# Two linear-attention and two gated-MLP layers on one Trainium2 core: K of layer two at one Strassen level, and a new order of the first loads, heads and prologues

## The chip, the cores and the metric

The kernel runs on one core of one Trainium2 chip. The metric is the device time of one execution in microseconds (us); the time of a kernel is the median of its runs. The core has five engines that the text names: TensorE (PE; its weight loads are PEld), VectorE (DVE), ScalarE (ACT), GpSimd (POOL) and SyncE (SP), which here issues every DMA. Matmuls write to PSUM, which has eight banks of 128 x 512 f32; everything else lies in SBUF, which the program holds as one tensor called `arena` (and PSUM as `ps`).

## The reference

S = 2048 tokens, D = 1024, 32 heads of 32, F = 3584. A is a linear attention without a mask, B a gated MLP without a nonlinearity, and each is applied twice with the same weights.

```python
def A(x, wqkv, wo):
    q, k, v = heads(x @ wqkv)
    phi = lambda t: jnp.where(t > 0, t + 1, jnp.exp(t)) + 1e-6
    pq, pk = phi(q), phi(k)
    kv = jnp.einsum("bhsd,bhse->bhde", pk, v)
    z = jnp.einsum("bhsd->bhd", pk)
    num = jnp.einsum("bhqd,bhde->bhqe", pq, kv)
    den = jnp.einsum("bhqd,bhd->bhq", pq, z)[..., None] + 1e-6
    return merge(num / den) @ wo

def B(x, w_gate, w_up, w_down):
    return ((x @ w_gate) * (x @ w_up)) @ w_down

x = x + A(layernorm(x)); x = x + B(layernorm(x))
x = x + A(layernorm(x)); x = x + B(layernorm(x))
```

## The kernel before, in words

All of x stays in SBUF as 16 token tiles of 128 (`x_res`, bf16). A layer norm is split over the engines (class `LN`, L508): statistics (L471 and L473 on VectorE, or L465 and L483 on ScalarE), the root on POOL (L474 and L476, or L467, L485 and L487), the scaled tile (L504 or L497 on VectorE), and the transposition into `xnT`, by TensorE with a copy of ScalarE (L596 and L598; L588 and L590 for tile 0) or by a DMA (L582). `flow_step` moves each of these on by one tile.

`layer_A` (L937) does attention in three stages. In the K and Q stage each tile of 128 tokens gets its K and Q: 8 matmuls of 512 columns for each half of 512 features. ScalarE takes the exponential of a PSUM bank (L657 in layer one, L1031 and L1027 in layer two), VectorE takes its minimum with 1 (L647 for K, L645 for Q) and joins it with the linear part (L662; L1040 and L1050 in layer two). For K, POOL then adds the tile to the sum z (`z_add`, L971, instructions L976 and L978). The G stage (L1291) multiplies normalized x by phi(K) over all tokens, and the stage with L1303, L1331 and L1383 makes V, the output projection and the residual.

In layer one K and Q use plain matmuls (L954), in the order of the list `seq`. The first two tiles do K only; in tiles 2 to 5 Q of the tile two back goes ahead of K, from tile 6 on K goes ahead of Q. Beside the K tiles from the fourth on, VectorE forms four sums of Q's weight blocks (`pt_ops`, L821 at 128 x 2048), which a DMA stores in `pt_scratch` for layer two.

In layer two `kq_pairs` (L997) works by pairs of token tiles. Every step has a position, and the steps are emitted in the order of their positions (L1173 to L1200). K is plain for all eight pairs (L945): four steps of 8 matmuls. Q is at one Strassen level for seven pairs (`strassen`, L1100; matmuls L1115): seven products of 4 matmuls in place of the eight of a plain pair. `st1` copies product 1 to a second bank (L1124), `st5` stores product 5 (L1130), `st6` and `st7` add that to a bank on VectorE (`join`, L1119), and each finished bank gets its phi. The Strassen products need sums of token blocks, which VectorE makes for two pairs at a time (`s_sums`, L1080, through L821 at 128 x 1024), and sums of weight blocks, which are loaded from `pt_scratch` (`load_t`). The phi of a step is emitted in that step. K uses banks 0 to 3 and Q banks 4 to 7, apart from the first pair.

Every engine's queue is in order. What reads and writes which bytes or banks is tracked by a recorder (`_Prog`), which puts a semaphore wait on each instruction that needs one; nothing is reordered after emission. So the order on each queue, SP's with its DMAs too, is the order in which the Python code emits.

`layer_B` (L1438) multiplies by gate, up and down weights with one Strassen level and, for some products, two (L1470, L1540, L2020, L1918; joins L1559). A part of the first pair's products, the prologue `pro`, is emitted ahead of the stage by `pro_step` (L1432), which pops one matmul group each time. In layer two one group goes between the last two output groups of attention (L1415), and in the second pass three go into product 3 of the down projection (L1952). Layer one has no prologue for its first pass (L1726).

## Time and profile before

| what | value |
|---|---|
| median of 3 runs | 1447.18 us (1445.64 to 1447.40) |
| the profiled execution's own time | 1446.97 us |
| its span, first to last instruction | 1445.2 us |
| instructions | 21993 |
| mean granted TensorE clock | 1.000 |
| DMA moved | 324.41 MB, mean 224 GB/s |
| K and Q stage of layer two, L945's start to L1291's | 98.3 us |

The profile page gives the busy time of each engine, the span in slices, the DMA queues, the chain of work that ended last and the costliest groups. `L945` is line 945 of the kernel before. In a timeline a row reads: start, length, engine, line, operation, out<-in, shape, count, and in brackets the idle time of the engine before it with what ended it. In a group row the figures after the bar are busy time, mean nanoseconds of one, and idle time before it. A row of waits reads: who waited for whom, us in total, times, the longest. A row of windows gives the length and, for PE, PEld, DVE, ACT and POOL, busy us and count, then the clock, the DMA share and GB/s. A row of DMA issues gives count, size of each and median us from issue to landing.

### The profile page before, as it was taken

Reading aid. Unit: us, or ns where it says so; the run is one execution under the profiler, and the core shown is the slowest. Engines: PE = TensorE matmul, PEld = TensorE weight load, DVE = VectorE, ACT = ScalarE, POOL = GpSimd, SP = SyncE. Lnnn points to the kernel's source line nnn. Section 1 sums busy time; section 2 is a strip of 40 time slices with the busy share of each in tenths; the row PEclk is TensorE's granted clock in tenths of the full one; section 3 lists DMA queues with packets and bytes.
Section 4 is the critical chain, followed back from the end, with each engine's and each line's share of the span. In section 5 each row is a group of like instructions: output and inputs, shape, how many; then the busy total and the mean of one; then the engine's idle time right before and its main releaser. Section 6 shows DMA issues by size and latency. Waiting matters only on the chain.

```text
span 1445.2 us, 21993 instructions
## 1 busy us (share of the span) xinstructions
PE 1433.9 (99%) x8294; PEld 800.4 (55%) x8294; DVE 1128.6 (78%) x2027; ACT 680.2 (47%) x1438; POOL 227.5 (16%) x260
## 2 busy tenths in 40 slices
PE   8999999999999999999999999999999999999999
PEld 3444444555544555554664444456666457666547
DVE  6766889889867799877677779879877786777856
ACT  3652256677720255550156423567777005777401
POOL 4543733000000000000044346300000000000000
PEclk9999999999999999999999999999999999999999
DMA  6334757987879899986896067679975779887657
GB/s 233 88 79 118 151 125 155 290 298 249 294 288 338 262 271 294 293 257 225 253 341 195 0 173 151 155 213 274 282 260 197 241 247 296 264 264 257 205 164 239
DMA packets 377993, 324.41 MB, mean 224 GB/s; under 512 B 178208, under 2 KB 326048, under 8 KB 377632
## 3 DMA queue, kind: packets, MB, share of 16 engines
q1 hardware_dynamic: 377888, 323.02, 74.5%
q8 instruction: 65, 1.06, 0.3%
q14 instruction: 40, 0.33, 0.1%
HBM read 237.24 MB, written 62.13 MB: 207 GB/s over the span
## 4 chain that ended last, share of the span: by engine, by line
PE 92%; DVE 4%; DMA 2%; ACT 1%; issue 0%; SPq 0%; POOL 0%; DVEq 0%
PE ps L1470 25%; PE ps L1540 17%; PE ps L2020 16%; PE ps L1291 8%; PE ps L954 6%; PE ps L1383 6%; PE ps L1918 6%; PE ps L945 4%; PE ps L1115 3%; DVE arena L821 2%; DVE arena L824 1%; DMA arena<-in_A_wqkv_dram 1%; DMA arena<-in_B_w_up_dram 1%; DMA arena<-in_B_w_down_dram 1%; PE ps L1303 0%
## 5 line engine op out<-in xcount | busy, mean ns | idle before, releaser
L821 DVE TENSOR_TENSOR arena<-arena 128x512 f16<-128x512 f16 (+7 forms) x752 | 414.1, 577 | 75.9 <-ACT arena L1584 47.6
L1470 PE MATMUL ps<-arena 128*128 128x512 f16 x1808 | 446.5, 379 | 0.7 <-ACT ps L1500 0.7
L824 DVE SCALAR_TENSOR_TENSOR arena<-ps,arena 128x512 f16<-128x512 f32 (+2 forms) x448 | 298.8, 686 | 76.0 <-PE ps L2020 52.2
L1540 PE MATMUL ps<-arena 128*128 128x256 f16 x2324 | 311.8, 273 | 1.7 <-DVE ps L1559 1.3
L1540 PEld LDWEIGHTS ps<-arena 128*128 128x128 f16 (+1 forms) x2324 | 226.2, 98 | 105.0 <-DVE ps L1559 5.8
L1470 PEld LDWEIGHTS ps<-arena 128*128 128x128 f16 (+1 forms) x1808 | 176.4, 98 | 141.8 <-ACT ps L1500 1.4
L2020 PE MATMUL ps<-arena 128*128 128x512 f16 (+1 forms) x1120 | 243.2, 379 | 0.0
L2020 PEld LDWEIGHTS ps<-arena 128*128 128x128 f16 x1120 | 109.6, 98 | 131.3
L1475 ACT ACTIVATE arena<-ps 128x512 f16<-128x512 f32 x224 | 134.0, 598 | 94.0 <-PE ps L1470 90.8
L1556 ACT COPY ps<-ps 128x256 f32<-128x256 f32 x220 | 81.1, 369 | 128.5 <-PE ps L1540 121.4
L1559 DVE TENSOR_TENSOR ps<-ps,arena 128x256 f32<-128x256 f32 x220 | 92.3, 428 | 36.5 <-PE ps L1540 18.4
L474 POOL TENSOR_SCALAR arena<-arena 128x1 f32<-128x1 f32 x48 | 19.5, 407 | 626.1 <-DVE arena L473 626.1
L954 PE MATMUL ps<-arena 128*128 128x512 bf16 x512 | 112.5, 379 | 3.8 <-DMA arena<-in_A_wqkv_dram 1.1
L1291 PE MATMUL ps<-arena 128*128 128x512 bf16 x512 | 115.4, 379 | 0.0
L1383 PE MATMUL ps<-arena 128*128 128x512 bf16 x512 | 111.0, 379 | 0.0
L1922 ACT COPY ps<-ps 128x256 f32<-128x256 f32 x32 | 11.4, 357 | 209.2 <-PE ps L1918 147.1
L1214 POOL TENSOR_TENSOR arena<-arena 128x1024 f16<-128x1024 f32 x32 | 79.2, 2476 | 70.2 <-DVE arena L1212 69.0
L1500 ACT COPY ps<-ps 128x512 f32<-128x512 f32 x112 | 64.2, 573 | 52.0 <-PE ps L1540 44.5
L1918 PE MATMUL ps<-arena 128*128 128x256 f16 (+1 forms) x784 | 87.0, 273 | 0.1
L978 POOL TENSOR_TENSOR arena<-arena 128x512 f32<-128x512 f32 x60 | 74.8, 1266 | 74.1 <-DVE arena L1040 44.0
L954 PEld LDWEIGHTS ps<-arena 128*128 128x128 f16 x512 | 49.5, 98 | 63.0 <-DMA arena<-in_A_wqkv_dram 1.6
L1383 PEld LDWEIGHTS ps<-arena 128*128 128x128 f16 x512 | 50.1, 98 | 60.2
(77 smaller groups left out, 1215.6 us busy)
## 6 DMA issues: line engine op xcount, KB each, us to landing
arena<-w_scratch SPq DMA_DIRECT2D x84, 512.0 KB, 4.9
arena<-sp_scratch SPq DMA_DIRECT2D x56, 512.0 KB, 5.8
arena<-t_scratch SPq DMA_DIRECT2D x29, 896.0 KB, 6.8
arena<-in_B_w_down_dram SPq DMA_DIRECT2D x21, 896.0 KB, 6.9
w_scratch<-arena SPq DMA_DIRECT2D x28, 512.0 KB, 6.5
sp_scratch<-arena SPq DMA_DIRECT2D x28, 512.0 KB, 4.1
arena<-in_B_w_gate_dram SPq DMA_DIRECT2D x42, 256.0 KB, 5.0
arena<-in_B_w_up_dram SPq DMA_DIRECT2D x42, 256.0 KB, 3.2
```

What stands on the lines that cost most here:

```text
L821: P.add("dve", lambda e: e.tensor_tensor(out=out, in0=a, in1=b, op=op), rd=rd, wr=wr, prd=prd)
L824: P.add("dve", lambda e: e.scalar_tensor_tensor(out=out, in0=a, scalar=sc, in1=b, op0=ALU.mult, op1=op1), rd=rd, wr=wr, prd=prd)
L954: return [e.matmul(psb(bank), xnT[:, k, i * 128:(i + 1) * 128], w[:, k, :], start=(k == 0), stop=(k == KT - 1)) for k in range(KT)]
L1291: return [e.matmul(psb(bank), xr[:, t, j * 128:(j + 1) * 128], pk[:, h, t, :], start=(t == 0), stop=(t == NST - 1)) for t in range(NST)]
L1383: return [e.matmul(psb(bank), xnT[:, g, i * 128:(i + 1) * 128], wp[:, g, dh * 512:(dh + 1) * 512], start=(dh == 0 and g == 0), stop=(g == ...
L1470: P.add("pe", lambda e: [e.matmul(psb(bank), w[:, k, :], x[:, k, :], start=(start and k == 0), stop=(k == 3), skip_group_check=True) for k ...
L1475: P.add("act", lambda e: e.activation(t, psb(bank), AF.Copy, scale=SG), prd=[bank], wr=r)
L1540: P.add("pe", lambda e: [e.matmul(psb(bank)[:, 256 * half:256 * half + 256], w[:, k, :], xx[:, k, :], start=(start and k == 0), stop=(k == ...
L1556: P.add("act", lambda e: e.copy(psb(dst[c])[:, 0:256], lo), prd=[bk], pwr=[dst[c]])
L1559: P.add("dve", lambda e: e.tensor_tensor(out=psb(dst[c])[:, 256:512], in0=lo, in1=c5, op=ALU.add), prd=[bk], rd=rc5, pwr=[dst[c]])
L1918: P.add("pe", lambda e: [e.matmul(psb(bank)[:, 256 * half:256 * half + 256], a[:, k, :], w[:, k, :], start=(start and k == 0), stop=(k == ...
L2020: return [e.matmul(psb(bank), hv[:, 7 * hf + k, t * 128:(t + 1) * 128], w[:, k, :], start=(start and hf == 0 and k == 0), stop=(hf == 1 an ...
```

## The change

- **First loads.** x tile 1 is loaded ahead of K's weights, and two tiles come ahead of the second half of Q's weights.
- **Early heads.** In layer one tiles 0 and 1 no longer go through `seq`. Their K is emitted by hand: half of tile 0's first half, the transposes of tile 1, the rest, tile 1's first half, the transposes of tile 2, then the second halves. Half of tile 1's statistics stands ahead of tile 0's scaling. From tile 2 on K always goes ahead of Q.
- **K at one Strassen level.** `KSTR` is on and `KP0` is 3, so pairs 3 to 7 of K go through `strassen`, with their phi by halves (`SEP = "qk"`). Layer one also forms and stores the sums of K's weights (`pt_ops("k")`, at tiles 9 to 13), and layer two loads them behind Q's. The second block of Q's plain weights, which only the last tiles use, is loaded behind the stage. The positions of Q, of the norm and of the sums are other ones; the sums for a pair stand earlier. There are three exponential buffers in place of four.
- **Phi one step later.** In `kq_pairs` the phi of a step (`fin1`, `fin2`) is put on a list and emitted behind the next K or Q step; the list is emptied ahead of the first step of a pair.
- **Prologues earlier.** Layer one's first pass gets a prologue of one group (`P1A` of pair 0), three output groups ahead of the end of attention. In layer two's first pass three groups go between the last output groups, and in the second pass four.

In numbers: 20 matmuls of 512 columns fewer (196 to 336 at L1115, 288 to 128 at L945); on VectorE 14 to 24 joins, 15 to 6 double phi (L1040), 30 to 48 single phi (L1050), 31 to 22 minima of 1024 and 2 to 20 of 512 (L647), 16 to 20 sums of 128 x 2048; on ScalarE 12 copies L1130 in place of 7, and 5 copies L1124 without a bias more.

```diff
-    KSTR = False
-    QLAG = 0.284
-    QEND = 0.102
-    SEP = "q"
-    LNP = (0.474, 0.5)
-    SPOS = 0.283
-    SSTEP = 0.14
+    KSTR = True
+    NEB = 3
+    KQ_SEQ = ""
+    QLAG = 0.409
+    QEND = 0.476
+    SEP = "qk"
+    LNP = (0.371, 0.594)
+    SPOS = 0.874
+    SSTEP = 0.119
...
-    KP0 = 1
+    KP0 = 3
...
             for h in range(2):
+                if h and mid is not None:
+                    mid()
                 P.add("dve", (lambda h: lambda e: e.bn_stats(...
...
-                OP5 = {"k": RC, "q": RC + 2048 if KSTR else RC + 2 * SZ_SLOT + 4096}
+                OP5 = {"k": RC, "q": RE + 6144 if KSTR else RC + 2 * SZ_SLOT + 4096}
...
+                pend, left = [], {}
+
+                def flush():
+                    while pend:
+                        pend.pop(0)()
...
-                def fin2(kind, i, eb, b0, b1, up):
+                def fin2(*a):
+                    pend.append(lambda: fin2_(*a))
+
+                def fin1(*a):
+                    pend.append(lambda: fin1_(*a))
...
-                            at(((p - SPOS if p else 0.05) if KSTR else p + 1 - SPOS) + SSTEP * n, f)
+                            at((p - SPOS if KSTR and p >= KP0 else p + 1 - SPOS) + SSTEP * n, "S%d%d" % (p, n), f)
...
-                for _, _, f in sorted(ev, key=lambda t: t[:2]):
-                    f()
+                for _, _, tk, f in run:
+                    if tk[0] not in "KQ":
+                        f()
+                        continue
+                    if tk[2] == "0":
+                        flush()
+                    n = len(pend)
+                    f()
+                    for _ in range(min(n, len(pend))):
+                        pend.pop(0)()
+                flush()
...
                 lnp.start(0)
-                lnp.b_one()
-                lnp.start(1)
+                lnp.start(1, lnp.b_one)
...
-            seq = [("k", i) for i in range(NHOLD)]
+            seq = []
             for i in range(NHOLD, NST):
-                pair = [("k", i), ("q", i - NHOLD)]
-                seq += pair[::-1] if first and i < NPE_T else pair
-            if not first:
+                seq += [("k", i), ("q", i - NHOLD)]
+            if first:
+                b0, b1, b2, b3 = next_banks(4)
+                kq_i[0] += 4
+                ev = [phi_evac(b, [k_dst(i, h) for h in range(2)]) for i, b in enumerate(((b0, b1), (b2, b3)))]
+                proj_kh(0, 0, b0, range(4))
+                lnp.step_t(1)
+                proj_kh(0, 0, b0, range(4, KT))
+                ev[0][0](0)
+                lnp.b_one()
+                lnp.start(3)
+                proj_kh(1, 0, b2)
+                ev[1][0](0)
+                lnp.step_t(1)
+                for i, b in enumerate((b1, b3)):
+                    proj_kh(i, 1, b)
+                    ev[i][0](1)
+                    ev[i][1]()
+                    z_add(i)
+                lnp.b_one()
+                lnp.start(4)
+            else:
                 kq_pairs()
                 seq = []
...
+                if not first and i == NST - 1:
+                    pro_step(pro, 1)
                 y_grp(tok[i], 0, i)
...
                 y_seed(i + 1)
+                if i == NST - 2 or not first and i == NST - 1:
+                    pro_step(pro, 1)
...
-                if i == NST - 1:
-                    pro_step(pro, 1)
                 y_grp(tok[i], 1, i)
...
-                npro = 0 if jit else [tk[:2] in early for _, tk in seq].index(False)
+                npro = [tk[:2] in early for _, tk in seq].index(False)
+                if jit:
+                    npro = 1
+                    seq.insert(0, seq.pop([tk for _, tk in seq].index("P1A+")))
...
-                            if q == "3" and i in (3, 4) and (i == 4 or p):
+                            if q == "3" and i in (3, 4):
                                 pro_step(pro, 1)
...
                     elif t == 1:
                         if KSTR:
-                            load_t("k", 0, 2)
+                            load_q(1, 1)
                     elif t == 2:
-                        if KSTR:
-                            load_t("k", 2, 2)
-                        else:
+                        load_t("q", 0)
+                        if not KSTR:
                             load_q(0, 0)
                             load_q(1, 0)
-                        load_q(1, 1)
-                        load_t("q", 0)
+                            load_q(1, 1)
                     else:
                         load_t("q", 1, 2)
                         load_t("q", 3)
-                        if not KSTR:
+                        if KSTR:
+                            load_t("k", 0, 2)
+                            load_t("k", 2, 2)
+                        else:
                             load_q(0, 1)
...
+        xload(1)
         load_w("k", 0)
-        xload(1)
+        xload(2)
         load_w("k", 1)
-        xload(2)
+        xload(3)
         load_w("q", 0)
-        xload(3)
+        xload(4)
+        xload(5)
         load_w("q", 1)
-        for i in range(4, NST):
+        for i in range(6, NST):
             xload(i)
```

More of the change, by code (lines that the diff above doesn't have):

```diff
@@ L533, in buf, with start @@
                 return n % 4 if (n < 10 if self.to == "B" else n >= 8) else n % 2
-            def start(self, i):
+            def start(self, i, mid=None):
                 assert i == self.n
                 act = self.stat_act
-                j = ln_a(self.order[i], act, self.o_junk)
+                j = ln_a(self.order[i], act, self.o_junk, mid)
                 self.n += 1
@@ L947, in proj2, with proj @@
                       rd=r_xT(i * 128, (i + 1) * 128) + rw[0] + rw[1], pwr=[bank])
[L949 to L951 removed]
+            def proj(w, rw, i, bank=None, ks=range(KT)):
+                if bank is None:
+                    bank = B_KQ[kq_i[0] % len(B_KQ)]
+                    kq_i[0] += 1
                 def fn(e):
                     return [e.matmul(psb(bank), xnT[:, k, i * 128:(i + 1) * 128], w[:, k, :],
[L955 removed]
+                                     start=(k == 0), stop=(k == KT - 1)) for k in ks]
                 P.add("pe", fn, rd=r_xT(i * 128, (i + 1) * 128) + rw, pwr=[bank])
@@ L966, in q_dst, with proj_kh @@
                 return x_res[:, i, h * 512:(h + 1) * 512], r_x(i, h * 512, (h + 1) * 512)
-            def proj_kh(i, h):
-                proj(wkh[first][h], R(O_WKH[first][h], 8192), i)
+            def proj_kh(i, h, bank=None, ks=range(KT)):
+                proj(wkh[first][h], R(O_WKH[first][h], 8192), i, bank, ks)
             def z_add(i):
@@ L1010, in bk @@
                 def bk(kind, p):
-                    r = ROLE[0 if kind == "k" and (p < KP0 or not KSTR) else p % 2]
+                    r = ROLE[0 if kind == "k" else p % 2]
                     return {n: BG["q" if p == 0 else kind][r[n]] for n in r}
```

63 lines of the change are left out of this document (37 added, 26 removed).

## The prediction

> **What bounds the kernel now.** I read the page's busy shares and its chain first, then TensorE's waits, then single stretches of the timelines.
>
> ```profile
> PE 1433.9 (99%) x8294; PEld 800.4 (55%) x8294; DVE 1128.6 (78%) x2027; ACT 680.2 (47%) x1438; POOL 227.5 (16%) x260
> PE 92%; DVE 4%; DMA 2%; ACT 1%; issue 0%; SPq 0%; POOL 0%; DVEq 0%
> ```
>
> TensorE (PE) is busy 99% of the span and holds 92% of the chain that ended last. So time changes in two ways only: fewer matmuls, or fewer and shorter gaps between them. Two pieces of the chain in order of time (start, length, line, count) price a matmul, and TensorE's own waits (total, times, longest) show the gaps; the others stand in the parts below.
>
> ```profile
> 737.16 10.51 PE ps L945 x48
> 835.48 6.91 PE ps L1291 x32
> PE ps L1115 <- DVE ps L1119: 0.2, 1, 0.2
> ```
>
> A 512-column matmul takes 6.91/32 = 0.216 us when nothing stops it. Idle time is counted from a modelled end (a row's last matmul lasts 379 ns), so each gap costs 379 - 216 = 0.16 us more than the rows show: 1.15 is 1.31 lost. The K and Q stage of layer two runs from 737.16 to 835.48, 98.3 us. It holds 256 plain and 196 Strassen matmuls, 452 x 0.216 = 97.6; only 0.7 us of it is gaps.
>
> **Part 1: the start of layer one (loads with x first, early heads).** The timeline, the issues and the chain from the start:
>
> ```profile
> 7.93 1.90 PE L954 MATMUL ps<-arena 128*128 128x512 bf16 x8 [0.94 <-ACT arena L590]
> 10.98 1.90 PE L954 MATMUL ps<-arena 128*128 128x512 bf16 x8 [1.15 <-DMA arena<-in_A_wqkv_dram]
> 12.72 0.61 PE L596 MATMUL ps<-arena 128*128 128x128 f16 x8
> 14.47 3.63 PE L954 MATMUL ps<-arena 128*128 128x512 bf16 x16 [1.15 <-ACT arena L598]
> 25.29 0.61 PE L596 MATMUL ps<-arena 128*128 128x128 f16 x8
> 5.77 0.55 DVE L504 TENSOR_SCALAR arena<-arena 128x1024 f16<-128x1024 bf16 x1 [1.00 <-POOL arena L476]
> 13.41 1.01 ACT L598 COPY arena<-ps 128x1024 f16<-128x1024 f16 x1
> arena<-in_A_wqkv_dram SPq DMA_DIRECT2D x1, 1024.0 KB, 5.5
> arena<-in_A_x_dram SPq DMA_DIRECT2D x1, 256.0 KB, 5.8
> 2.80 8.13 DMA arena<-in_A_wqkv_dram
> 1.71 0.43 SPq L433 DMA_DIRECT2D arena<-in_A_wqkv_dram  x1
> 2.18 0.58 SPq L433 DMA_DIRECT2D arena<-in_A_x_dram  x1
> 3.10 1.42 DVE L471 BATCH_NORM_STATS2 arena<-arena 128x6 f32<-128x512 bf16 x2 [3.10 <-DMA arena<-in_A_x_dram]
> ```
>
> Two gaps of 1.31 us follow the first half-projection: the second half of K's weights lands at 10.93, and tile 1 waits for its transposed copy. Nothing else is queued on TensorE to fill them.
>
> Loads land in the order of issue: K's first half, issued 1.71, lands at 7.2; x tile 1, issued 2.18, at 8.0; K's second half at 10.93. A tile is about 0.8 us of queue, 1 MB about 2.9. With tile 1 ahead, it lands about 0.8 us behind tile 0 (3.10), near 4.0, and K's first half near 8.0, 0.1 us later than TensorE needs it (7.93). K's second half, behind one more tile, lands near 11.7.
>
> On VectorE (DVE) half of tile 1's statistics (0.71) moves into the 1.0 us in which L504 waits for GpSimd (POOL): no cost if tile 1 has landed by 5.0. The rest of tile 1's chain then ends with L504 about 2.5 us after tile 0's, at 8.8. TensorE: four matmuls 8.0 to 8.9, transposes of tile 1 to 9.3 (about 0.45, from the 12.72 row and its successors), four matmuls to 10.2, then a wait for the copy (0.7 after the transposes' start, 1.01 long) to 10.65. Then tile 1's first half to 12.4, transposes of tile 2 to 12.8, both second halves to 16.3, K of tile 2 to 19.75, transposes of tile 3, Q of tile 0 to 23.65. Before, the same work (with the transposes that start at 25.29) ends at 25.74. **Gain 2.1 us**; bounds: 2.6 with both gaps wholly gone, 0 if later weights and the copy give as much back. Q's halves (near 15.4 and 19.8) are needed at 20.2 and 21.9.
>
> ```profile
> 61.87 2.32 PE L954 MATMUL ps<-arena 128*128 128x512 bf16 x10 [0.55 <-DVE arena L662]
> 51.81 1.80 DVE L821 TENSOR_TENSOR arena<-arena 128x2048 f16<-128x2048 bf16 x1
> 81.47 0.55 DVE L497 TENSOR_SCALAR arena<-arena 128x1024 f16<-128x1024 bf16 x1 [2.46 <-POOL arena L487]
> ```
>
> The gap at 61.87 (0.55 + 0.16) has its origin where the old order put K of tiles 5 and 6 back to back; the new order alternates from the start, so Q's eviction gets 3.45 us more. I count **0.7 us** (bounds 0 and 0.7). Layer one also makes K's four weight sums: four L821 of 1.80 us, for tiles 9 to 12, and a 2 MB store. In these tiles VectorE waits 2.46 us for GpSimd anyway, so they cost nothing; were that cover gone, at most 4 x 1.8 on VectorE. SP's store goes out two tiles (13.8 us) before V's load queues behind it.
>
> **Part 2: a prologue product earlier at the start of layer one's MLP.**
>
> ```profile
> 243.89 0.82 PE L1470 MATMUL ps<-arena 128*128 128x512 f16 x3 [0.67 <-ACT ps L1500]
> 283.25 0.83 PE L1540 MATMUL ps<-arena 128*128 128x256 f16 x6 [0.74 <-DVE ps L1559]
> 260.48 4.62 DVE L821 TENSOR_TENSOR arena<-arena 128x256 f16<-128x256 bf16 x10 [1.34 <-DMA arena<-in_B_w_up_dram]
> ```
>
> P1A's four matmuls go 24 matmuls ahead, so its copy (L1500) is done and the 0.83 us at 243.89 goes. But what is late next is VectorE, which runs on weight loads here (1.34 us at 260.48) and holds TensorE at 283.25. VectorE's order is unchanged, so TensorE reaches 283 earlier and waits longer. I count **0**; bounds 0 and -0.8.
>
> **Part 3: K of layer two.** Pairs 3 to 7 go from 32 to 28 matmuls: 5 x 4 x 0.216 = **4.3 us** less, all on TensorE's path. What this adds lies on the other engines:
>
> ```profile
> 736.90:780.00 43.10, 42.87 (x199) 19.05 (x197) 32.13 (x48) 30.96 (x56) 24.77 (x34) 1.00 0.89 274
> 780.00:835.50 55.50, 55.50 (x258) 25.02 (x257) 39.64 (x58) 25.25 (x43) 20.36 (x18) 1.00 0.18 56
> L1050 DVE SCALAR_TENSOR_TENSOR arena<-ps,arena 128x512 bf16<-128x512 f32 x15 | 10.3, 688 | 4.1 <-ACT arena L1027 3.9
> L1040 DVE SCALAR_TENSOR_TENSOR arena<-ps,arena 128x1024 bf16<-128x1024 f32 x7 | 8.6, 1224 | 0.2
> L1119 DVE TENSOR_TENSOR ps<-ps,arena 128x512 f32<-128x512 f32 x8 | 5.5, 689 | 0.0
> L647 DVE TENSOR_SCALAR arena<-arena 128x1024 bf16<-128x1024 bf16 x6 | 2.5, 422 | 1.9 <-ACT arena L1031 1.8
> L645 DVE TENSOR_SCALAR arena<-arena 128x512 bf16<-128x512 bf16 x4 | 1.2, 291 | 6.1 <-ACT arena L1031 6.1
> ```
>
> From 780 VectorE is busy 39.64 of 55.5 us, 9.25 per pair of steps (60 matmuls, 12.95 us). A Strassen pair of K loses 2 x (0.42 + 1.22) = 3.3 us of phi and gets 4 x (0.29 + 0.69) and two joins of 0.69, 5.3: VectorE's pair becomes 11.25 us, TensorE's 56 x 0.216 = 12.1. ScalarE, busy 25.25 of 55.5 us, gets two copies more per pair. So VectorE goes to 93%, with the sums (L821) unevenly in pairs 3 and 5, where it is over 100% for some microseconds. A join has 2.6 us (three other steps of 0.86) until TensorE needs it, 0.9 of it its own; a lag of over 1.7 us stalls TensorE. For it speaks that phi is now queued one step later: before, VectorE sat in front of phi for ScalarE (6.1 us before L645, 4.1 before L1050) with a join behind. Against it is a collision on GpSimd:
>
> ```profile
> 830.92 1.22 DVE L647 TENSOR_SCALAR arena<-arena 128x512 bf16<-128x512 bf16 x1 [0.67 <-ACT arena L1031]
> 829.72 2.27 POOL L978 TENSOR_TENSOR arena<-arena 128x512 f32<-128x512 f32 x2 [2.83 <-DVE arena L1040]
> ```
>
> A half phi minimum, 0.29 us alone, took 1.22 beside the z sum and ended 0.15 us after it. K's tiles now end 1.73 us apart and a z sum lasts 2.27, so about one minimum per pair is caught: 0.93 us, VectorE's pair 12.2, against 12.1. I take gaps of 1.1 us for the stage in place of 0.7: **-3.9 us**. Bounds: -5.0 with no gap; three catches per pair (14.0 on VectorE, 5 x 1.9 lost) +4.7.
>
> [...]
>
> The loads: K's four blocks (2 MB) go ahead of the stash and the transposes, Q's last block (0.5 MB) goes behind the stage. The queue is full:
>
> ```profile
> arena<-pt_scratch SPq DMA_DIRECT2D x1, 1024.0 KB, 9.5
> 759.57 1.49 SPq L582 DMA_TRANSPOSE arena<-arena  x1
> arena<-arena SPq DMA_TRANSPOSE x1, 3.8
> ```
>
> 1.5 MB more at the start's 2.9 us per MB, and one reload of 0.25 MB more ahead, is about 5.1 us: the fourth transpose (759.57 + 3.8) lands near 768.5 instead of 763.4. The sums for pair 4 now need it at step position 3.13, 737.2 + 12 x 1.73 + 13 x 0.86 = 769.1, and VectorE arrives 1 to 2 us later: no cost, with 1.6 to 2.6 us to spare. Past that each microsecond stalls VectorE, joins behind it.
>
> **Part 4: prologue of layer two's MLP.**
>
> ```profile
> 961.76 1.92 PE L1540 MATMUL ps<-arena 128*128 128x256 f16 x14 [0.55 <-DVE ps L1559]
> 963.83 1.49 PE L1540 MATMUL ps<-arena 128*128 128x256 f16 x12
> 1203.26 1.92 PE L1540 MATMUL ps<-arena 128*128 128x256 f16 x14
> 1205.33 1.48 PE L1540 MATMUL ps<-arena 128*128 128x256 f16 x12
> ```
>
> Product 1's three steps now stand between groups of eight 0.216 us matmuls, so the join wait at 961.76 (0.71) goes, and of the 0.55 lost inside each block (2.07 for 14 x 0.108) the second join, 0.2. **-0.9 and -0.2** (bounds: 0 and -1.6 together). Between the two places TensorE's waits show nothing of this size, so nothing late swallows it.
>
> **Sum.** -2.1 - 0.7 + 0 - 3.9 - 0.9 - 0.2 = -7.8 us. The profiled execution took 1446.97 us (span 1445.2 and 1.8 around it), 0.2 under the median of the three runs, 1447.18. Forecast from the median: **1439.4 us**.
>
> **Rivals.**
> - VectorE becomes the bound of pairs 3 to 7 by collisions with GpSimd (slower). It breaks even where 5 x (11.25 + 0.93 n - 12.1) = 7.8 + 1.1, at n = 2.8 catches of the five minima in a pair. At all five VectorE needs 15.9 us a pair, 19 us lost less the 1.1 counted: 1457. For: the 1.22 row. Against: GpSimd is busy only 20.36 of 55.5 us. Chance 0.06, slower in two thirds of it.
> - Most of the Strassen gain goes into gaps behind late joins or the late transpose: 3.4 us more, 1442.8. For: 93% on VectorE, in-order. Chance 0.2.
> - The start gains nothing, because the first weights or tile 1 land later: 1441.5. Chance 0.1.
> - Part 2's gap is also won, and the stage has no gaps: 1437.5. Chance 0.12.
> - Forecast: 0.52, between 1438.3 and 1441.
>
> 0.2% (2.9 us) is about what a measurement of this kernel can tell from no change. Faster (below 1444.3): 0.52 + 0.2 x 0.9 + 0.1 + 0.12 = 0.92, taken as 0.89 since the rows come from one execution. Same 0.07, slower 0.04. The range 1436.8 to 1443.4 leaves out the first rival and the outer parts of two others.
>
> **What would show it.** Start: no wait of L954 for weights, Q of tile 0 done near 23.7. No gap near 60. At 280 a gap of 1.5 us or more (mine) or under 1 (the fourth rival). L945 to L1291 of 94.4 us; L1119 as releaser of at most 1.1 us, and L647 at 512 columns with a mean under 0.55. No gap of 0.5 near 955. I am wrong if that stage exceeds 96 us, or if the start keeps a gap over 1 us.

## The result, and the profile after

The changed kernel takes **1442.07 us** (median of 5 runs, 1441.05 to 1442.24) against 1447.18 (1445.64 to 1449.32, 5 runs) before: a ratio of 0.9961, 95% interval 0.9948 to 0.9975. It is faster by 0.4%. The forecast was 1439.4 us: the sign is right and the time lies in the range, 2.7 us above the forecast. The profiled execution took 1442.1 us, with a span of 1440.0.

The busy shares and the shares of the chain that ended last, from the page of the changed kernel:

```profile
PE 1430.2 (99%) x8274; PEld 799.4 (56%) x8274; DVE 1144.7 (79%) x2059; ACT 686.1 (48%) x1448; POOL 230.0 (16%) x260
PE 95%; DVE 2%; DMA 2%; SPq 0%; ACT 0%; issue 0%
```

TensorE has 20 matmuls fewer and still bounds the kernel. To see where the 5.2 us of span come from, one lays the same piece of work of the two chains side by side. First the kernel before (start, length, engine, line, count):

```profile
117.29 6.91 PE ps L1291 x32
...
252.42 8.03 DMA arena<-in_B_w_up_dram
...
270.92 7.62 DMA arena<-in_B_w_down_dram
...
1120.26 48.36 PE ps L2020 x224
```

Then the changed kernel, where L1291, L2020 and L945 have become L1349, L2083 and L949:

```profile
116.01 6.91 PE ps L1349 x32
...
250.87 8.59 DMA arena<-in_B_w_up_dram
...
269.90 8.20 DMA arena<-in_B_w_down_dram
...
736.70 10.36 PE ps L949 x48
...
830.92 6.91 PE ps L1349 x32
...
1115.05 48.36 PE ps L2083 x224
```

Up to the G stage of layer one the change wins 1.28 us (117.29 to 116.01). Up to the K and Q stage of layer two it gives 0.82 back: that begins at 736.70 in place of 737.16, only 0.46 earlier. The stage itself is 94.22 us long in place of 98.32: 4.10 won. Layer two's MLP prologue brings 0.65 more (1120.26 to 1115.05 is 5.21), and the rest nothing. The chain shows where the second step loses: it runs over the same two weight loads as before, and both take longer from issue to landing, 8.59 in place of 8.03 us (w_up) and 8.20 in place of 7.62 (w_down). That is 1.14 us together, against 0.27 won on the way from the G stage to the first of them.

TensorE's timeline shows each part of the change (start, length, line, shape, count, and in brackets the idle time ahead with what ended it):

```profile
8.23 1.18 PE L959 MATMUL ps<-arena 128*128 128x512 bf16 x4 [1.27 <-DMA arena<-in_A_wqkv_dram]
...
10.05 3.91 PE L959 MATMUL ps<-arena 128*128 128x512 bf16 x12
...
257.26 0.83 PE L1600 MATMUL ps<-arena 128*128 128x256 f16 x6 [0.41 <-DVE ps L1619]
261.85 1.47 PE L1530 MATMUL ps<-arena 128*128 128x512 f16 x6 [0.52 <-ACT arena L1535]
282.80 0.83 PE L1600 MATMUL ps<-arena 128*128 128x256 f16 x6 [1.29 <-DVE ps L1619]
...
784.02 6.22 PE L1140 MATMUL ps<-arena 128*128 128x512 f16 x28 [0.56 <-DVE ps L1144]
...
958.62 1.49 PE L1600 MATMUL ps<-arena 128*128 128x256 f16 x12 [0.43 <-ACT arena L1644]
```

The gaps of the old start and the one at 61.87 are gone. The odd row is 10.05: 12 matmuls that should take 12 x 0.216 + 0.16 = 2.75 us take 3.91, with no wait between them. The gap at 243.89 is gone too, but there are two new ones at 257 and 262, and the one at 283 has grown from 0.74 to 1.29.

Why the start came short is in the windows (length; busy us and count of PE, PEld, DVE, ACT, POOL; TensorE's granted clock; DMA share; GB/s):

```profile
5.60:9.00 3.40, 1.54 (x13) 0.87 (x13) 2.07 (x5) 1.07 (x2) 0.90 (x3) 0.99 1.08 366
9.00:12.40 3.40, 3.40 (x16) 1.74 (x14) 1.98 (x4) 1.41 (x2) 0.79 (x2) 0.50 1.09 356
```

For 3.4 us, from 9.0 to 12.4, the granted clock was 0.50, and the 5 matmuls of 512 columns that started from 10.05 to 11.76 stood 0.427 us apart in place of 0.216. Four of the five runs have a mean clock of 0.999.

### The profile page after: what moved, and what is told of

Its sections match the earlier page's. It is cut to its first block, busy times and chain, and to the rows that moved or that the text cites. A ratio compares the mean times of both kernels' runs of the same rounds, so it can differ in the third digit from the quotient of the medians.

```text
span 1440.0 us, 22015 instructions
## 1 busy us (share of the span) xinstructions
PE 1430.2 (99%) x8274; PEld 799.4 (56%) x8274; DVE 1144.7 (79%) x2059; ACT 686.1 (48%) x1448; POOL 230.0 (16%) x260
## 4 chain that ended last, share of the span: by engine, by line
PE 95%; DVE 2%; DMA 2%; SPq 0%; ACT 0%; issue 0%
PE ps L1530 26%; PE ps L1600 17%; PE ps L2083 16%; PE ps L959 8%; PE ps L1441 8%; PE ps L1349 8%; PE ps L1981 6%; PE ps L1140 5%; PE ps L949 2%; DVE arena L825 1%; DVE arena L828 1%; DMA arena<-in_B_w_up_dram 1%; DMA arena<-in_B_w_down_dram 1%; PE ps L1361 0%; PE ps L1389 0%; DMA arena<-in_A_wqkv_dram 0%
## 5 line engine op out<-in xcount | busy, mean ns | idle before, releaser
L825 DVE TENSOR_TENSOR arena<-arena 128x512 f16<-128x512 f16 (+8 forms) x756 | 419.6, 581 | 76.9 <-ACT arena L1644 47.6
L2083 PE MATMUL ps<-arena 128*128 128x512 f16 (+1 forms) x1120 | 243.2, 379 | 0.0
L2083 PEld LDWEIGHTS ps<-arena 128*128 128x128 f16 x1120 | 109.6, 98 | 131.3
L1349 PE MATMUL ps<-arena 128*128 128x512 bf16 x512 | 115.4, 379 | 0.0
L1441 PE MATMUL ps<-arena 128*128 128x512 bf16 x512 | 111.5, 379 | 0.0
L983 POOL TENSOR_TENSOR arena<-arena 128x512 f32<-128x512 f32 x60 | 78.8, 1334 | 65.6 <-DVE arena L1073 34.0
L1441 PEld LDWEIGHTS ps<-arena 128*128 128x128 f16 x512 | 50.1, 98 | 59.8
```

Of the source, the lines that this page charges most:

```text
L825: P.add("dve", lambda e: e.tensor_tensor(out=out, in0=a, in1=b, op=op), rd=rd, wr=wr, prd=prd)
L1349: return [e.matmul(psb(bank), xr[:, t, j * 128:(j + 1) * 128], pk[:, h, t, :], start=(t == 0), stop=(t == NST - 1)) for t in range(NST)]
L1441: return [e.matmul(psb(bank), xnT[:, g, i * 128:(i + 1) * 128], wp[:, g, dh * 512:(dh + 1) * 512], start=(dh == 0 and g == 0), stop=(g == ...
L2083: return [e.matmul(psb(bank), hv[:, 7 * hf + k, t * 128:(t + 1) * 128], w[:, k, :], start=(start and hf == 0 and k == 0), stop=(hf == 1 an ...
```

## The experiments

Theory after the result: the terms of the forecast hold at full clock. What is missing at the end is (a) the stretch at half clock at the start, (b) the landing of the second w_down load near 278, which VectorE waits for and TensorE behind it, and which is not the same in every execution. Rivals: the start's order, or the new prologue, or a VectorE that is too full, costs the time by the way the code is ordered. All kernels below are edits of the changed kernel, and each was also run several times beside the kernel before on the same chip, except the one without the z sum, which has one time. In most profiles of the experiments some 50 matmul records are missing, so their starts and releasers are read, not their counts.

| kernel | median us (range, runs) | ratio to before, 95% interval |
|---|---|---|
| changed, once more | 1440.56 (1439.82 to 1441.40, 5) | 0.9955 [0.9942, 0.9969] |
| dummy matmuls at the start | 1442.00 (1439.24 to 1443.32, 5) | 0.9955 [0.9942, 0.9967] |
| no prologue in layer one | 1441.39 (1439.90 to 1441.98, 5) | 0.9952 [0.9940, 0.9965] |
| old start | 1443.58 (1442.08 to 1444.27, 6) | 0.9968 [0.9956, 0.9980] |
| phi not delayed | 1445.97 (1443.93 to 1447.65, 11) | 0.9986 [0.9978, 0.9995] |
| K plain (no Strassen for K) | 1445.34 (1442.79 to 1446.88, 11) | 0.9980 [0.9971, 0.9989] |
| six pairs of K at Strassen | 1443.81 (1441.51 to 1446.34, 8) | 0.9973 [0.9963, 0.9984] |
| no z sum in layer two | 1441.58 (1) | |
| early w_down loads | 1441.20 (1440.60 to 1442.45, 5) | 0.9961 [0.9948, 0.9973] |
| early w_down and dummies | 1439.57 (1438.74 to 1440.87, 5) | 0.9948 [0.9935, 0.9960] |
| the same, no prologue | 1440.46 (1439.40 to 1441.35, 5) | 0.9948 [0.9935, 0.9962] |
| early w_down, dummies, six pairs | 1440.75 (1440.39 to 1443.71, 5) | 0.9958 [0.9946, 0.9971] |

Differences of 1 us between two of these lie inside the intervals, so the traces decide. The second table cuts every trace at the first matmul of a stage (us): A from the first projection to the G stage, B from there to the K and Q stage of layer two, of that B' the piece from V's last stage (L1441, or L1383 before) to the first down projection, C the K and Q stage of layer two.

| trace | first projection at | A | B | B' | C |
|---|---|---|---|---|---|
| before | 7.93 | 109.19 | 619.87 | 221.22 | 98.33 |
| changed | 8.23 | 107.62 | 620.70 | 222.04 | 94.22 |
| changed, once more | 8.22 | 106.36 | 620.04 | 221.38 | 94.01 |
| dummies | 8.65 | 106.36 | 621.74 | 223.09 | 94.08 |
| no prologue | 8.61 | 106.36 | 620.55 | 221.89 | 94.70 |
| old start | 7.92 | 109.32 | 620.35 | 221.69 | 95.03 |
| phi not delayed | 8.40 | 107.62 | 619.45 | 220.80 | 98.22 |
| K plain | 8.12 | 106.37 | 619.47 | 220.81 | 97.56 |
| six pairs | 8.69 | 107.61 | 619.26 | 220.62 | 97.39 |
| no z sum | 8.59 | 107.61 | 620.90 | 222.24 | 93.50 |
| early w_down | 8.59 | 107.60 | 619.29 | 220.63 | 94.45 |
| early w_down, dummies | 9.55 | 106.36 | 619.10 | 220.45 | 94.66 |
| the same, no prologue | 8.25 | 106.36 | 618.84 | 220.18 | 95.41 |
| the three together | 8.32 | 106.36 | 618.59 | 219.94 | 96.25 |

### The start: dummies, the old start, and the same kernel again

```diff
                 lnp.start(1, lnp.b_one)
                 lnp.step_t(1)
+                P.add("pe", lambda e: [e.matmul(psb(B_KVT[1]), wrm[:, 0:128], wrm, start=True, stop=True) for _ in range(5)],
+                      rd=R(O_A[0], 1024), pwr=[B_KVT[1]])
```

> Adds five unused 512-column matmuls on TensorE between the transposes of tile 0 and the first K matmuls, where the changed kernel's TensorE sits idle from 6.8 to 8.2 us. Theory (the start lost 1.1 us because TensorE's clock was cut to half from about 9.0 to 12.4 us, after a stretch that was mostly idle): clock 1.000 over the span in every run, no 427 ns spacing between matmuls near 10 to 12.5, the G stage starts near 114.8 in place of 115.84, 1441.0 us. Rival (the slow stretch comes from loads landing beside the matmuls, or hits at random whatever TensorE does): the half clock stays, 1442.1.

The old start puts the old order of loads and the old `seq` back (and takes out the K steps of tiles 0 and 1 that were emitted by hand):

```diff
...
-            seq = []
+            seq = [("k", i) for i in range(NHOLD)]
             for i in range(NHOLD, NST):
-                seq += [("k", i), ("q", i - NHOLD)]
+                pair = [("k", i), ("q", i - NHOLD)]
+                seq += pair[::-1] if first and i < NPE_T else pair
...
+        load_w("k", 0)
         xload(1)
-        load_w("k", 0)
+        load_w("k", 1)
         xload(2)
-        load_w("k", 1)
...
```

> Undoes the loads with x first and the early heads, all else as changed. Theory (the two together gave 1.28 us: 0.6 in the start and 0.7 from the gap at 61.87, which came from K of tiles 5 and 6 standing back to back): both 1.31 us gaps and the gap near 62 are back, clock 1.000, the G stage starts near 117.1, 1443.4. Rival (the gap near 62 depended on something else that changed, and the start lost more than it won): no gap near 62, 1442 or less.

The changed kernel was also run again without an edit.

> The changed kernel once more, nothing edited. Theory (what TensorE loses between 240 and 290 us is set by when the second w_down load lands, and that landing differs from execution to execution): the profiled execution shows another gap near 283 than the 1.45 us of the first one, anywhere from 0.2 to 3, and the load's time from issue to landing differs from 8.20 us by several tenths; the stretch from the G stage's first matmul to the K and Q stage of layer two differs from 620.70 by up to 1.3 us. Rival (the gap belongs to the order of the code): the gap is again 1.45 within 0.2 and the stretch 620.7 within 0.3. Either: median 1441.0 to 1442.5, K and Q stage of layer two 94.2 within 0.5.

Its median, 1440.56, is below the expected 1441.0 to 1442.5; the gap near 283 and the w_down load follow in the next part. A takes only two values with the new start, 106.36 and 107.6, and 1.25 us lies between them. The windows of the second execution of the same code are the test:

```profile
5.60:9.00 3.40, 1.82 (x13) 1.08 (x13) 2.10 (x5) 1.07 (x2) 0.96 (x3) 1.00 1.05 366
9.00:12.40 3.40, 3.16 (x22) 1.53 (x20) 1.95 (x4) 1.51 (x2) 0.79 (x2) 1.00 1.09 358
```

The same instructions, now at a clock of 1.00, and A is 1.26 us shorter. So the code alone does not bring the half clock. It was there in 5 of the 8 profiled executions that have the new start without dummies and in none of the 4 with them. The mean clock of a run, which has three digits, points the same way: 1.000 in 19 of 20 runs with dummies and in 22 of 51 runs of the kernels with the new start and without them (1.25 us is one thousandth of the span). In 52 runs of the kernel before on the same chips it was 1.000 in 32, though its profile and that of the old start show A without a half clock; what lowers it in the others no trace shows.

Each trace also records when the clock rises. In all 14 the first matmuls, from 1.36 us on, stand about 0.43 us apart until the record of full clock begins, which is between 4.50 and 6.89 us: at 5.55 and 6.89 in the two executions of the changed kernel. (Ahead of that the windows read 1.00 because nothing is recorded.) The 3.41 us from the rise, for the changed kernel, its second execution and the dummies:

```profile
5.55:8.96 3.41, 1.55 (x13) 0.86 (x13) 2.03 (x5) 1.07 (x2) 0.94 (x3) 1.00 1.08 366
6.89:10.30 3.41, 2.43 (x22) 1.33 (x19) 2.24 (x6) 1.65 (x3) 0.79 (x2) 1.00 1.08 370
5.07:8.48 3.41, 2.08 (x15) 0.85 (x13) 1.95 (x4) 1.07 (x2) 1.36 (x4) 1.00 1.06 371
```

TensorE's busy time in this stretch sorts all 14 traces. In the five that lose the clock right behind it, for the next 3.41 us, it is 1.17 to 1.55 us; in the nine that keep it, before and the old start among them, it is 1.85 to 2.48. With the new start and no dummies the rise comes at 4.64 to 5.55 us in the five and at 6.51 to 6.89 in the other three, late enough for the stretch to take in more of the first projection. With the dummies it comes at 4.50 to 5.65, mostly as early as in the five, and the clock stays. So with the new start the clock fell where the kernel had no dummies and the rise came at 5.55 us or earlier, in five traces of five, and in none of the other seven. Why the rise moves, and whether the busy time itself decides, no trace shows.

The length of 3.41 us is read from the profiled execution of the changed kernel: its windows have a clock of 1.00 from 5.55 to 8.96, 0.50 from 8.96 to 12.37, and 1.00 from 12.37 to 16.00. TensorE was not wholly idle ahead of the fall: it was busy 1.55 us there, and 1.17 to 1.55 of the 3.41 us in the five traces.

The dummies' median did not fall by the 0.8 to 1.3 us that the start won: B is 621.74 in that trace, the longest of all. That is the next question. With the old start all three gaps are back (1.44 and 1.31 at 11.1 and 14.6, 0.71 at 62.0, counted with the modelled 0.16) and A of 109.32.

### Where 0.8 to 2.5 us go between 240 and 290

```diff
-                npro = [tk[:2] in early for _, tk in seq].index(False)
-                if jit:
-                    npro = 1
-                    seq.insert(0, seq.pop([tk for _, tk in seq].index("P1A+")))
+                npro = 0 if jit else [tk[:2] in early for _, tk in seq].index(False)
```

> Undoes the earlier prologue group of layer one's first MLP pass alone. Theory (TensorE waits near 283 for VectorE, which hangs on DMA landings, whatever it does before): the 0.83 us gap near 242 comes back, the gaps near 257, 262 and 283 (0.57, 0.68 and 1.45 us) shrink by as much, 1442.1, within 0.4. Rival (the earlier group itself made the 0.83 us that this stretch lost): the down projection starts 0.8 us earlier, 1441.2.

Without the prologue the gap of 0.83 is back at 241.74, the one at 257 is gone, the one near 262 is down to 0.2 and the one near 282 to 1.3 (0.57, 0.68 and 1.45 in the changed kernel, all with the modelled 0.16). B' is 221.89 in place of 222.04, so the rival's 0.8 us is not there. The median is 0.7 below the expected one, and so outside its 0.4; all five of its runs have a mean clock of 1.000.

VectorE's timeline near 276, first of the changed kernel, then of its second execution, then with the dummies:

```profile
278.12 2.62 DVE L825 TENSOR_TENSOR arena<-arena 128x1024 f16<-128x1024 bf16 x4 [1.99 <-DMA arena<-in_B_w_down_dram]
```

```profile
275.97 2.62 DVE L825 TENSOR_TENSOR arena<-arena 128x1024 f16<-128x1024 bf16 x4 [1.25 <-DMA arena<-in_B_w_down_dram]
```

```profile
277.97 2.62 DVE L825 TENSOR_TENSOR arena<-arena 128x1024 f16<-128x1024 bf16 x4 [3.45 <-DMA arena<-in_B_w_down_dram]
```

In all three VectorE is done with its work and sits until the second w_down load has landed. The chains give that load's time from issue to landing: 8.20, 7.54 and 8.49 us, and 7.01 with phi not delayed, where the edit is 450 us later:

```profile
269.79 7.01 DMA arena<-in_B_w_down_dram
```

The same load at the same place of the same queue takes 7.0 to 8.5 us, and TensorE's gap near 282 follows: 0.26, 0.72, 1.45 and 2.92 us (with 0.16 for the modelled end). Between the two executions of the changed kernel nothing differs but the execution, so the code does not fix this gap. With the dummies the load was also issued late: the SP queue took 6.59 us (262.86 to 269.45) for what stands ahead of it, 5.36 in the second execution. Moving the load is the test:

```diff
-                    elif u % 4 == 0:
-                        if j:
-                            wd_store(j - 1)
-                        if j < NJ // 2:
-                            wd_load(j)
+                    elif u % 4 == 3:
+                        if j + 1 < NJ // 2:
+                            wd_load(j + 1)
+                    elif u % 4 == 0:
+                        if j:
+                            wd_store(j - 1)
+                        else:
+                            wd_load(0)
```

> Changed kernel with each w_down load after the first issued one product earlier in layer one's first pass, behind the sums that read the buffer and ahead of the weight loads and the store that it stood behind. Theory (the second w_down load at 278 holds VectorE and through it TensorE, and swallows what is won before it): VectorE's wait for w_down near 278 (1.99 us) and the gap near 283 (1.45) go; the stretch from the G stage to the K and Q stage of layer two falls from 620.7 to 619.2 to 619.8, the median to about 1440.8. Rival (the queue's throughput is the limit, not one load's place): the load that now lands later, w_up near 259 to 266, holds VectorE in its place; a gap of over 1 us appears between 262 and 275, and the stretch and the median stay within 0.5 us of the changed kernel's.

```profile
276.23 2.61 DVE L825 TENSOR_TENSOR arena<-arena 128x1024 f16<-128x1024 bf16 x4
```

The wait is gone, and no other load takes its place there (the wait for w_up near 259 is 1.32 us, as it was): B' is 219.94 to 220.63 in the four kernels with the early load, 220.62 to 223.09 in the nine that have the load where the changed kernel has it. The theory holds against the rival of a full queue. The median of this kernel alone is no lower than that of the changed kernel beside it (1441.20 and 1440.56): its five runs have a mean clock of 0.998 and 0.999, four of the other five 1.000. With both causes taken away:

> The same early w_down loads, and five dummy matmuls of 512 columns behind tile 0's transposes, so that TensorE does not idle ahead of its first projection. Theory (full clock is worth 0.83 us at the start, and it was swallowed only by the w_down load): both gains now reach the end, granted clock 1.000, G stage begins near 115.0, the stretch to the K and Q stage 619.2 to 619.8, median about 1440.0, 0.8 below the kernel with early w_down loads alone. Rival (another wait behind the stage swallows it): G stage near 115.0, but the stretch is 0.8 us longer and the median the same as without the dummies.

It has the lowest median of the study, 1439.57 us; the G stage begins at 115.91, 0.9 late, because here the first weights landed late (first projection at 9.55). Against the changed kernel on the same chip the intervals overlap (0.9948 and 0.9955), so 1.0 us better is likely, not shown.

Is the prologue worth anything?

> Early w_down loads and five dummy matmuls as in the fastest kernel so far (1439.57, ratio 0.9948 to the kernel before), but without layer one's MLP prologue. Theory (the prologue trades the 0.83 us wait at its own place for later waits of about the same sum): the gap of 0.83 near 242 is back, the ones near 257 and 262 shrink to 0.2 together, the stretch to the K and Q stage stays within 0.4 us of 619.1, ratio 0.9945 to 0.9953. Rival (the prologue's gain was only swallowed by the late w_down load): the stretch is 0.8 us longer, 619.9, ratio 0.9953 to 0.996.

Without it the gap of 0.83 near 242 is the only one from 200 to 300; with it and the early load there are 0.44 and 0.64 (257 and 262), and with the dummies as well 0.91 at 257. B stays within 0.3 us of 619.1, and the ratio is 0.9948 again. The prologue trades one wait for others of the same sum, as forecast.

### The stage: what Strassen, the late phi and the collisions are worth

K plain again, with the positions of before (and so without K's weight sums, their store and their loads):

```diff
-    KSTR = True
-    NEB = 3
+    KSTR = False
+    NEB = 4
...
```

> Changed kernel with K of layer two plain for all eight pairs again, with the positions and the four exponential buffers of before; start, late phi and prologues stay changed. Theory (the stage's gain is the 20 matmuls, less what late joins give back): the K and Q stage of layer two takes 97.6 to 98.4 us in place of 94.2, the median is 3.4 to 4.2 above the changed kernel, 1444.5 to 1446. Rival (part of the gain is the late phi, which alone closes the 0.7 us of gaps that the stage had before, and the Strassen products alone bring less): stage 97.6 and no gap above 0.15 us in it, median near 1444.5.

C is 97.56 us, about 452 x 0.216, and no gap is left. The stage has the steps and positions of before, and differs in the late phi and in the order of some loads; so the late phi closes the 0.7 us of gaps that the stage had before (that the loads have no part in it is not shown), and Strassen on top saves 20 x 0.216 = 4.32 and costs about 1.0 in new gaps: 94.2. Now the other way round, Strassen without the late phi:

```diff
-                    pend.append(lambda: fin2_(*a))
+                    fin2_(*a)
...
-                    pend.append(lambda: fin1_(*a))
+                    fin1_(*a)
```

> Emits phi of layer two's K and Q in its own step again, all else as changed. Theory (putting phi one step later is what lets VectorE take the five Strassen pairs of K, since joins no longer stand behind a phi that waits for ScalarE): gaps on joins of 3 us or more in the K and Q stage in place of 0.85, the stage 96.5 to 98 us in place of 94.2, 1444.5 to 1446. Rival (VectorE has room in any order): stage within 0.5 us of 94.2, 1442.1.

TensorE's waits from 736 to 836 (who for whom, us, times, longest), first with phi not delayed, then of the changed kernel:

```profile
PE ps L1140 <- DVE ps L1144: 3.1, 6, 1.1
```

```profile
PE ps L1140 <- DVE ps L1144: 0.6, 1, 0.6
```

L1144 is the join. Without the late phi TensorE's matmuls wait for it six times, and C is 98.22: the 20 matmuls bring nothing. The late phi is worth 4.0 us here, nearly all of the stage's gain.

No z sum:

```diff
-                    if kind == "k":
-                        z_add(i)
+                    pass
...
-                    if z:
-                        z_add(i)
+                    pass
```

> Changed kernel without the z sum in layer two's K and Q stage: GpSimd does not add K's tiles there, so layer two's denominator lacks that sum. First rival of the prediction (minima of VectorE are caught by GpSimd's z sum, and that decides the stage): the stage falls from 94.2 to about 93.4 us, and the mean of the minima L647 at 512 columns falls toward 0.29 us. Theory (collisions happen, but VectorE has enough slack in these pairs): L647's mean falls, and the stage stays at 94.2 within 0.3; its gaps near 784 (0.7 us, a late join) stay within 0.3.

The changed kernel around its one gap, at 784, and the same place without the z sum:

```profile
780.03 3.61 POOL L983 TENSOR_TENSOR arena<-arena 128x512 f32<-128x512 f32 x3 [1.29 <-DVE arena L1073]
780.19 0.69 DVE L1073 SCALAR_TENSOR_TENSOR arena<-ps,arena 128x512 bf16<-128x512 f32 x1
...
781.39 1.24 DVE L649 TENSOR_SCALAR arena<-arena 128x512 bf16<-128x512 bf16 x1
782.66 0.69 DVE L1073 SCALAR_TENSOR_TENSOR arena<-ps,arena 128x512 bf16<-128x512 f32 x1
783.27 0.69 DVE L1144 TENSOR_TENSOR ps<-ps,arena 128x512 f32<-128x512 f32 x1
```

```profile
781.38 0.28 DVE L649 TENSOR_SCALAR arena<-arena 128x512 bf16<-128x512 bf16 x1
781.70 0.69 DVE L1072 SCALAR_TENSOR_TENSOR arena<-ps,arena 128x512 bf16<-128x512 f32 x1
782.31 0.69 DVE L1142 TENSOR_TENSOR ps<-ps,arena 128x512 f32<-128x512 f32 x1
```

A minimum of Q (L649) starts while GpSimd runs three z sums and takes 1.24 us in place of 0.28. The join behind it comes 0.96 later, and TensorE waits 0.72. Without the z sum C is 93.50, and no gap is left but one of 0.37 for a weight load near 739. C alone could not show this, for it runs from 94.01 to 95.41 in the eight traces in which this stage is unedited; but the gap at this place is in all eight (0.72 or 0.73), and only here is it gone. The rival of the expectation had the 93.4, though by the minima of K, which take 0.28 or 0.29 us in both kernels, and my own expectation of no change was wrong: collisions cost 0.7 us of this stage, at one place.

A sixth pair shows how near the edge VectorE is:

```diff
-    KP0 = 3
+    KP0 = 2
```

> Changed kernel with a sixth pair of K at one Strassen level (pairs 2 to 7): 4 matmuls fewer. Theory (VectorE still has slack, since taking the z sum away gained only 0.7 us): stage 93.3 to 93.8 us in place of 94.2, median 0.4 to 0.9 below the changed kernel. Rival (VectorE or the sums for the early pair, which need the weight sums and the transposes sooner, become late): a gap of over 1 us at a join or ahead of the first Strassen product of K, stage 94.2 to 96, median the same or up to 2 us longer.

TensorE's timeline, most of the rows with a wait:

```profile
738.40 8.81 PE L949 MATMUL ps<-arena 128*128 128x512 bf16 x40 [0.95 <-DMA arena<-in_A_wqkv_dram]
...
771.10 1.04 PE L1140 MATMUL ps<-arena 128*128 128x512 f16 x4 [1.08 <-DVE ps L1144]
772.67 2.76 PE L1140 MATMUL ps<-arena 128*128 128x512 f16 x12 [0.54 <-ACT ps L1151]
775.97 9.67 PE L1140 MATMUL ps<-arena 128*128 128x512 f16 x44 [0.54 <-DVE ps L1144]
...
786.21 4.06 PE L1140 MATMUL ps<-arena 128*128 128x512 f16 x18 [0.57 <-DVE ps L1144]
```

Four matmuls fewer (0.86) and C is 97.39, 3.2 us longer. Of these 1.1 is a weight load that came late; the rest is late joins and a late copy of ScalarE (L1151) from 754 to 786, the largest of them shown. With the two other edits:

> The sixth pair of K at one Strassen level, the early w_down loads and the five dummy matmuls together. If all three add up: 0.4 to 0.9 below the kernel with the last two (1439.57), so 1438.7 to 1439.2, stage 93.3 to 93.8 and a granted clock of 1.000. If the sixth pair is late, as its rival has it: 1439.5 to 1441.5.

C is 96.25, and the ratio 0.9958 is no better than the changed kernel's. So the sixth pair is late, as the rival had it, both times; the stage came out longer than the rival's 94.2 to 96 us.

## Why the prediction was right and wrong

**Start: -2.1 and -0.7 forecast, -1.28 measured; this is the step that failed.** The gap at 61.87 went as counted. The order of the work was right almost to the digit: from a first projection at 8.0 to the G stage the forecast has 106.3 us (117.12 - 2.8 - 8.0, with before's first matmul of the G stage at 117.12), and every trace with the new start at full clock has 106.36 or 106.37. What failed is the price: each matmul was counted at 0.216 us, and in the profiled execution 3.4 us ran at half clock, which lost 1.26. A further 0.23 is K's weights, 8.23 in place of 8.0. At full clock (the second execution) the G stage begins 2.54 us earlier than before, against 2.8, and Q of tile 0 is done at 23.9 (its row starts at 20.45, and 16 x 0.216 is 3.45), against 23.7 in the prediction; in the profiled execution it is done at 25.2. That 3.4 us of the start could run at a clock of 0.50 was in none of my bounds; the lower bound of 0 covered it by number, not by reason.

**Part 2: 0 forecast, 0.83 lost.** "What is late next is VectorE, which runs on weight loads" is what happened: the two loads on the chain took 1.14 us longer than before. The bounds, 0 and -0.8, were one-sided: I took the landing of a load as fixed, and it moves by 1.5 us between executions. In eight traces with that order the piece B' runs from 220.62 to 223.09, before is 221.22 and without the prologue 221.89, so the 0.83 is within this spread and is not shown to be a cost of the prologue. My sign for it, a gap at 280 of 1.5 or more against under 1, could not tell the cases apart: the same code gave 1.45 and 0.72.

**Part 3: -3.9 forecast, -4.1 measured.** The stage took 94.22 (forecast 94.4) and 94.01, though unedited stages in other traces reach 95.41. The gaps counted at 1.1 are 0.9 (94.22 less 432 x 0.216). The reason was half right. One of K's minima per pair beside a z sum, as I counted it, is what the kernel with phi not delayed shows; this is the first of five such rows in its timeline of VectorE, 0.87, 0.87, 0.87, 0.87 and 0.68 us long:

```profile
780.67 0.87 DVE L651 TENSOR_SCALAR arena<-arena 128x512 bf16<-128x512 bf16 x1
```

In the changed kernel K's minima start ahead of a z sum or behind it, all 20 take 0.28 or 0.29 us, and it is Q's minima that are caught. The late phi, which I named only as an argument for a join in time, moved them clear; without it 0.1 us of the stage's gain is left.

In the changed kernel the rows show the two engines meeting: L649 started at 781.39, while GpSimd ran a z sum (781.14, 1.34 us long), took 1.24 us in place of 0.28 and ended at 782.63, 0.15 us after that sum. This did not make the first rival come true, because one catch alone delayed a join past its time.

**Part 4: -0.9 and -0.2 forecast, -0.65 and 0 measured.** The join's wait of 0.55 at 961.76 is gone, and in its place ScalarE's copy L1644 is late, 0.43 at 958.62, and in the second place 0.37 at 1200.11. I had not asked what follows the join.

**Sum.** The span fell by 5.2 us against 7.8 forecast: 1.5 of the 2.6 is the start, 0.8 part 2, 0.45 part 4, less 0.2 won in part 3. In the second execution of the same code the span is 1437.8, 7.4 less than before. So the forecast was near that of a good execution, and it was 1.2 and 2.7 us below the two medians, because nothing in it stood for what differs between executions. The time lies outside the 1438.3 to 1441 to which the forecast gave a chance of 0.52. In number it is nearest to the rivals at 1441.5 (the start gains nothing) and 1442.8 (the Strassen gain goes into gaps), but neither happened: the start gained 1.28 us and was held back by the clock more than by a load, and the stage gained more than forecast.

What stays open: why the clock rises at 4.5 us in one execution and at 6.9 in another, what makes the w_down load take 7.0 or 8.5 us, and whether the z sums can be moved away from Q's minima, which wasn't tried.

## What to carry to other kernels

When a kernel is 99% on one engine, count matmuls for the gain and then ask for each whether the consumers can follow: here a delay of one step for phi was worth all of a Strassen level, and one pair more than VectorE could serve cost more than it saved. Gains of 1 us ahead of a wait for a DMA are kept or lost by that landing, which here took 7.0 to 8.5 us for the same load at the same place, so give such a load an earlier place first, and profile the same code twice before a gap is put down to an edit. Where TensorE idles ahead of its first long stretch (1.27 us in the changed kernel), look at the granted clock in that stretch (0.50 for 3.4 us), in more than one execution.

## What the runs showed of the hardware

VectorE's groups from 780 to 830, changed kernel and without the z sum (busy us, mean ns, idle ahead):

```profile
L1073 DVE SCALAR_TENSOR_TENSOR arena<-ps,arena 128x512 bf16<-128x512 f32 x33 | 22.6, 688 | 3.3 <-ACT arena L1042 2.6
...
L651 DVE TENSOR_SCALAR arena<-arena 128x512 bf16<-128x512 bf16 x17 | 4.9, 286 | 2.7 <-ACT arena L1046 2.7
L649 DVE TENSOR_SCALAR arena<-arena 128x512 bf16<-128x512 bf16 x5 | 3.8, 756 | 0.0
L825 DVE TENSOR_TENSOR arena<-arena 128x1024 f16<-128x1024 f16 x4 | 3.5, 868 | 0.0
```

```profile
L1072 DVE SCALAR_TENSOR_TENSOR arena<-ps,arena 128x512 bf16<-128x512 f32 x35 | 24.2, 690 | 3.8 <-ACT arena L1042 3.0
...
L825 DVE TENSOR_TENSOR arena<-arena 128x1024 f16<-128x1024 f16 x4 | 2.7, 682 | 0.0
L649 DVE TENSOR_SCALAR arena<-arena 128x512 bf16<-128x512 bf16 x5 | 1.4, 283 | 0.0
```

Of these groups only the ones whose operands all lie in SBUF grow beside GpSimd: L649 from 283 to 756 ns, L825 from 682 to 868. L651 keeps its time (286 and 287), as it starts ahead of a z sum or behind it. L1073, which reads PSUM as well, does not grow (688 and 690), and the one at 780.19 took 0.69 wholly beside a z sum. The second surprise, half the clock for 3.4 us near the start of some executions of the same code, is shown with the experiments: it followed where TensorE was busy 1.17 to 1.55 us in the 3.41 us behind the clock's rise, and did not where it was busy 1.85 to 2.48.
